# Attention rounds of a fused attention and mixture-of-experts kernel: another order of rows, transposes, evictions and sums, and an earlier start of the first expert slot's gathers

## The chip, the cores and the metric

The kernel runs on one core of one Trainium2 chip. The metric is the time of one execution on the device, in microseconds (us). Besides the timed runs there is one profiled execution, whose instructions, waits and transfers can be looked at one by one.

## What is computed

The reference has two parts. The first is attention in chunks: 8 batches, 8 heads and 576 positions of 64 numbers; each chunk of 64 positions sees only itself. The second is a layer of 8 experts: each of the 4608 rows (8 heads of 64 numbers side by side, 512 in all) goes to the one expert with the largest logit.

```python
scores = scale * np.matmul(q_c, k_c.transpose(0, 1, 2, 4, 3))
scores = scores - np.max(scores, axis=-1, keepdims=True)
attn = np.exp(scores)
attn = attn / (np.sum(attn, axis=-1, keepdims=True) + 1e-09)
out = np.matmul(attn, v_c)
...
logits = x @ w_gate + modality_bias[modality_id]
e_idx = np.argmax(logits, axis=1)
gate_w = probs[np.arange(N), e_idx]
for e in range(E):
    mask = e_idx == e
    h = np.maximum(x[mask] @ w1[e], 0.0)
    out[mask] = gate_w[mask, None] * (h @ w2[e])
```

## The kernel before, in words

The 4608 rows are 36 tiles of 128. The program order of every engine is written out by hand, so each engine runs its own queue in just the order in which the code emits instructions; waits between engines are semaphores.

**A tile of attention** passes through these helpers. `scores` multiplies q and k on TensorE (PE) into `sp` in PSUM, takes the maximum on VectorE (DVE, line 249) and subtracts it (line 251). `exps` takes the exponential `ex` on ScalarE (ACT, line 256), and GpSimd (POOL) adds its two halves into `sr` (line 257). `sums` adds these up on DVE (lines 261, 262) to the reciprocal `ris`. `transposes` turns `ex` on PE (line 268) and ACT evicts it as `at` (line 270). `values` multiplies with v on PE (line 282) and ACT evicts `xt` (line 285). `rows` turns the product back on PE (line 294, which also gives the gate's logits) and DVE scales it into `xr` (line 296). `put` copies the logits `lp` on ACT (line 306) and stores `xr` to the array `xd` in DRAM, by a DMA that ACT issues (line 307).

**A round** handles two tiles, a and a+1, from a = 2 to 34. In before it is, on PE: transposes of a, rows of a-2 and of a-1, transposes of a+1, scores of a+2 and a+3, values of a and a+1. PSUM has eight banks: four for the pair `yb`, two under the tag "s" (for `sp`) and two under "t" (for `ap`, `xp`). The exponential of a+2 is emitted straight behind the scores, the one of a+3 behind both values. Loads of v are held until a transpose of the round is done.

**Routing.** The first 14 tiles are group 0. In the rounds behind them `route` works out each row's place (DVE, POOL, and two matmuls into `rp`, line 364), and `scatter` writes 14 times 128 rows into the table `tab` (POOL indirect DMAs, line 385), one per call of `advance`. `early_table` picks the first three expert slots. `locate` then reads a slot's list from the table into `tl` (SP DMA, line 523); it waits until all 14 scatters have landed. `gather` copies the row numbers to `tk` (POOL, line 540) and fetches the rows from `xd` into `xg` (POOL indirect DMAs, line 544, one for each 128 rows). `split` transposes `xg` on PE (line 584), and ACT and DVE split it into a high and a low part (lines 585, 586).

**The table PLAN** says what of the first slot's preparation follows the values of which tile: the key k stands for tile 36 + k. "locate" and "gather" are as above, "fetch" loads weights, "hi" and "lo" split them (ACT line 612, DVE line 616).

**The expert slots** follow: 13 sure ones and a few that depend on the input. In each, eight steps of `first` (line 641) and `second` (line 654) keep PE at work. The last tile's rows are taken inside slot 0 by `last`.

Of the kernel before, what the change touches and what calls it, by code (L numbers as in the profile page):

```python
# [8 lines left out]
F32 = mybir.dt.float32  # L9
# [13 lines left out]
E = 8  # L23
# [11 lines left out]
BUSY = 4  # L35
PLAN = {
    -9: {"fetch": [(0, 1), (1, 1)]},
    -7: {"locate": [(0,), (1,), (2,)]},
# [51 lines left out]
def attention_moe(ctx: ExitStack, tc: tile.TileContext, qkv, mod, cst, bias, wcat, wfst, out):  # L90
# [23 lines left out]
    def load_v(t, hold=None):  # L114
        if t < NT:
            b = wk.tile([P, DM], F32, name="v", bufs=NV)
            d = SP.dma_start(b, qkv[t][:, 2])
            if hold is not None:
                after(d, [hold.ins.name], "loads of v while the whole array works")
            st[t]["v"] = b  # L120
# [60 lines left out]
    def clear_part():  # L181

        i = len(clears)
        if i < 2 * E:
            a, n = (0, low_rows) if i < E else (low_rows, CAP - low_rows)
            m = ROW * n // P
            w = SP.dma_start(tabe[i % E:i % E + 1, ROW * a:ROW * (a + n)].rearrange("e (p m) -> p (e m)", p=P),
                            oob[:, 0:m])
            apart(w, "tab")
            clears.append(w)  # L190
# [63 lines left out]
    def exps(t):  # L254
        ex = st[t]["ex"]
        A.activation(ex, ex, AF.Exp, scale=0.125)  # L256
        G.tensor_tensor(sring[t % 4][:, :, 0:32], ex[:, :, 0:32], ex[:, :, 32:64], ALU.add)  # L257

    def sums(t):
        sm = wk.tile([P, H], F32, name="sm")  # L260
        V.reduce_sum(sm, sring[t % 4], axis=AX.X)  # L261
        V.reciprocal(ris[:, t], sm)

    def transposes(t):
        ex = st[t]["ex"].rearrange("p h k -> p (h k)")
        ap = ps.tile([P, NP, P], F32, tag="t", name="ap")
        for p in range(NP):
            hold = PE.transpose(ap[:, p, :], ex[:, p * P:p * P + P], ident)  # L268
        at = mp.tile([P, DM], F32, tag="yo", name="at", bufs=4).rearrange("p (a c) -> p a c", a=NP)
        A.copy(at, ap)  # L270
        st[t]["at"] = at
        return hold
# [15 lines left out]
    def rows(t):  # L288
        xt, ri = st[t]["xt"], ris[:, t]

        xr = wk.tile([P, NJB, NK, 32], F32, name="xr", bufs=4)
        fp = yb[t % 2].rearrange("p b (a c) -> p (b a) c", a=2)
        for p in range(NP):
            PE.matmul(fp[:, p, 0:GWC], xt[:, p, :], gw[:, p, :], start=True, stop=True)  # L294
        rb = ri.rearrange("p (a b) -> p a b", a=NP).unsqueeze(3)
        V.tensor_tensor(  # L296
            xr.rearrange("p (b j) a d -> p a b j d", b=2),
            fp[:, :, 0:P].rearrange("p a (b j d) -> p a b j d", b=2, j=2),
            rb.unsqueeze(4).to_broadcast([P, NP, 2, 2, 32]), ALU.mult)
        st[t] = fp, xr  # L300

    def put(t):
        fp, xr = st.pop(t)
        g = next(i for i, (a, n) in enumerate(GROUPS) if a <= t < a + n)
        lp = lps[g % 2][:, t - GROUPS[g][0]]
        A.copy(lp.rearrange("p (a b) d -> p a (b d)", a=NP), fp[:, :, P:GWC])
        A.dma_start(xd[t * P:(t + 1) * P, :], xr.rearrange("p j c d -> p (j c d)"))
# [4 lines left out]
    def route(g):  # L312
        t0, n = GROUPS[g]
        ts = slice(t0, t0 + n)

        def tl(name, dt=F32, bufs=1):
            return wk.tile([P, n, E], dt, name=name, bufs=bufs)


        l0 = lps[g % 2][:, 0:n]  # L320
        (G if g < NEG else V).tensor_tensor(
            l0, l0, ris[:, ts].unsqueeze(3).to_broadcast([P, n, H, E]), ALU.mult)
        yield
        lh = wk.tile([P, n, H // 2, E], F32, name="lh", bufs=1)
        lg = tl("lg")
        G.tensor_tensor(lh, l0[:, :, 0:4], l0[:, :, 4:8], ALU.add)
        G.tensor_tensor(lh[:, :, 0:2], lh[:, :, 0:2], lh[:, :, 2:4], ALU.add)
        G.tensor_tensor(lg, lh[:, :, 0], lh[:, :, 1], ALU.add)
        G.tensor_tensor(lg, lg, mb[:, ts], ALU.add)
        for _ in range(1 if g < NEG else 5):  # L330
            yield
        mx = wk.tile([P, n], F32, name="gmx")
        V.reduce_max(mx, lg, axis=AX.X)
        V.tensor_tensor(lg, lg, bc(mx, n), ALU.subtract)
        ge = tl("ge")
        A.activation(ge, lg, AF.Exp)
        va = tl("va")
        V.scalar_tensor_tensor(va, lg, 0.0, rev.unsqueeze(1).to_broadcast([P, n, E]), ALU.is_equal, ALU.mult)
        fm = wk.tile([P, n], F32, name="fm")
        V.reduce_max(fm, va, axis=AX.X)  # L340
        yield

        off = OFF
        oh = tl("oh", BF16)
        V.tensor_tensor(oh, va, bc(fm, n), ALU.is_equal)
        V.tensor_copy(scan[0][:, off + 1:off + 1 + n], oh)
        d = 1
        i = 0
        while d < n:
            if d == 4:  # L350
                yield
            a, b = scan[i], scan[1 - i]
            V.tensor_tensor(b[:, off + 1:off + 1 + n], a[:, off + 1:off + 1 + n],
                            a[:, off + 1 - d:off + 1 - d + n], ALU.add)
            d, i = 2 * d, 1 - i
        gs = wk.tile([P, n], F32, name="gs")
        V.reduce_sum(gs, ge, axis=AX.X)
        V.tensor_scalar_add(gs, gs, 1e-9)
        tg = tgs[g]
        V.reciprocal(tg.bitcast(F32)[:, :, 1], gs)  # L360
        for _ in range(2 if g < NEG else 5):
            yield
        rp = ps.tile([P, 2, 32, E], F32, tag="t", name="rp")
        PE.matmul(rp[:, 0, 0:n], ub, oh, start=True, stop=True)
        PE.matmul(rp[:, 1, 0:n + 1], ones, scan[i][:, off:off + n + 1], start=True, stop=True)
        V.tensor_tensor(base[g + 1], base[g], rp[:, 1, n], ALU.add)
        ra = tl("ra")
        V.tensor_tensor(ra, rp[:, 0, 0:n], base[g].unsqueeze(1).to_broadcast([P, n, E]), ALU.add)
        V.tensor_tensor(ra, ra, rp[:, 1, 0:n], ALU.add)
        V.tensor_tensor(ra, ra, oh, ALU.mult)  # L370
        pf = wk.tile([P, n], F32, name="pf")
        V.reduce_sum(pf, ra, axis=AX.X)
        pi = cp.tile([P, n], I32, name=f"pi{g}")
        V.tensor_copy(pi, pf)
        if g == NEG - 1:
            jobs.append(early_table())
        elif g == len(GROUPS) - 1:
            jobs.append(slot_table())
        pooljobs.append(scatter(g, pi, tg))
# [198 lines left out]
    def split(k, tag="t"):  # L578

        hi, lo = xring[0]  # L580
        tp = ps.tile([P, 512], F32, tag=tag, name="tp")[:, 0:SLOT]
        for t in range(NTT):
            assert ("rows", 0, t) in ready
            PE.transpose(tp[:, t * P:(t + 1) * P], xg[:, t, k * P:(k + 1) * P], ident)
        A.copy(hi[:, k], tp)
        V.tensor_tensor(lo[:, k], tp, hi.bitcast(F32)[:, k], ALU.subtract)  # L586
# [153 lines left out]
    busy(BUSY)  # L740

    for a, n in [(0, 1), (1, 1)] + [(t, 2) for t in range(2, NT, 2)]:
        hold = transposes(a)
        if a > 1:
            for t in (a - 2, a - 1):
                rows(t)
                sums(t + 2)
                put(t)
            load_v(a + 2, hold)
            if 8 <= a < 24:  # L750
                clear_part()
            load_v(a + 3, transposes(a + 1))
            if 8 <= a < 24:
                clear_part()
            for g, (t0, m) in enumerate(GROUPS):
                if t0 + m == a:
                    jobs.append(route(g))
        else:
            if not a:
                exps(1)  # L760
            sums(a)
        advance([pooljobs])
        small = [t for t in (range(a + 2, a + 4) if a > 1 else (a + 2,)) if t < NT]
        for t in small:
            scores(t)
            load_qk(t + NB)
        if n == 2 and small:
            exps(a + 2)
        advance([pooljobs])
        for t in range(a, a + n):  # L770
            values(t)
            if small and (n == 1 or t > a):
                exps(small[-1])
            advance()
            plan(t - NT)
        if a == 2:
            prepare()
    split(0, "s")
    rows(NT - 2)
    split(1, "s")  # L780
    put(NT - 2)
    split(2)
    split(3)
# [81 lines left out]
```

## Time and profile before

| what | value |
|---|---|
| timed runs | 563.55, 566.1 and 566.12 us, median 566.1 |
| the profiled execution | 564.9 us, of it 563.1 us span |
| PE busy | 548.5 us, 97% |
| DVE busy | 360.9 us, 64% |
| ACT busy | 244.7 us, 43% |
| POOL busy | 173.7 us, 31% |
| granted clock of PE | 0.996 |

The span reaches from the first to the last instruction of the program. In a timeline a row is: start in us, duration in us, engine, line, operation, tiles (written<-read), shapes, count, and in brackets the idle time of the engine before it with what ended it. In the chain of waits a row is start, duration, and what the end of the program waited for at that time. An engine name with q is its sequencer, which issues DMAs. Ends of matmuls are modelled, so rounds are best measured from start to start.

### The profile page before, as it was taken

What the parts mean: (1) busy time and instruction counts of PE and PEld (TensorE: products, weight loads), DVE (VectorE), ACT (ScalarE), POOL (GpSimd) and SP (SyncE); (2) the same over time, 40 slices, a digit from 0 to 9 for tenths busy, and PEclk for the clock granted to TensorE, in tenths of its full rate; (3) what the DMA queues carried; (4) which work ended last, traced back from release to release, by engine and by line L of the source; (5) the groups of instructions that cost most, each with busy time, mean ns of one, the idle gap of its engine ahead of it and who ended that gap; (6) DMA issues with size and microseconds to landing.
All of it is one profiled execution on the core that took longest, in us unless ns stands there. A gap on an engine that the chain in (4) does not pass through costs nothing.

```text
span 563.1 us, 12401 instructions
## 1 busy us (share of the span) xinstructions
PE 548.5 (97%) x4900; PEld 497.6 (88%) x4900; DVE 360.9 (64%) x633; ACT 244.7 (43%) x422; POOL 173.7 (31%) x182
## 2 busy tenths in 40 slices
PE   8999999999999999999999999999999999999994
PEld 5999999988889899899898998998898998998993
DVE  4767798967899665655656565565655646556751
ACT  3455555556534433433434434343434434445531
POOL 3322526733558753031220402213032210402001
PEclk9999999999999999999999999999999999999998
DMA  8889999989788649787683876758486673757400
GB/s 329 317 299 320 357 343 324 303 295 366 224 267 264 211 141 312 260 242 219 166 306 125 265 248 195 252 138 286 175 262 230 177 259 113 233 186 234 161 37 26
DMA packets 61410, 133.22 MB, mean 237 GB/s; under 512 B 11231, under 2 KB 31391, under 8 KB 54945
## 3 DMA queue, kind: packets, MB, share of 16 engines
q1 hardware_dynamic: 48368, 103.08, 56.3%
q0 software_dynamic: 7072, 19.18, 10.3%
q10 hardware_dynamic: 5904, 10.11, 4.9%
q8 instruction: 40, 0.66, 0.5%
q14 instruction: 26, 0.20, 0.1%
HBM read 102.16 MB, written 30.70 MB: 236 GB/s over the span
## 4 chain that ended last, share of the span: by engine, by line
PE 73%; issue 13%; DVE 5%; POOL 3%; ACT 2%; DMA 2%; ACTq 0%; POOLq 0%; DVEq 0%
PE yb L654 29%; PE hp L641 28%; PE yb L294 5%; PE xp L282 5%; PE sp L247 4%; PE ap L268 2%; DVE xr L296 1%; POOL out L666 1%; DMA out<-yo,tk 1%; DVE ex L251 1%; DMA qk<-in_qkv 1%; DVE mx L249 1%; ACT ex L256 1%; DVE sm L261 1%; POOL xg L544 0%
## 5 line engine op out<-in xcount | busy, mean ns | idle before, releaser
L616 DVE TENSOR_TENSOR wl<-raw,wh 128x1024 fp32r<-128x1024 f32 (+1 forms) x106 | 129.6, 1224 | 37.2 <-ACT wh L612 37.1
L644 ACT ACTIVATE hh<-hp 128x384 fp32r<-128x384 f32 (+1 forms) x104 | 49.3, 474 | 217.8 <-PE hp L641 215.0
L641 PE MATMUL hp<-xl,wh 128*128 128x384 f32 (+1 forms) x416 | 136.5, 328 | 0.0
L641 PE MATMUL hp<-xh,wh 128*128 128x384 f32 (+1 forms) x416 | 136.2, 327 | 0.0
L641 PE MATMUL hp<-xh,wl 128*128 128x384 f32 (+1 forms) x416 | 136.2, 327 | 0.0
L645 DVE SCALAR_TENSOR_TENSOR hl<-hp,hh 128x384 fp32r<-128x384 f32 (+1 forms) x104 | 55.7, 536 | 111.1 <-ACT hh L644 111.0
L654 PE MATMUL yb<-wh,hl 128*128 128x512 f32 x296 | 117.3, 396 | 0.5 <-DVE hl L645 0.5
L654 PE MATMUL yb<-wh,hh 128*128 128x512 f32 x296 | 117.4, 397 | 0.0
L654 PE MATMUL yb<-wl,hh 128*128 128x512 f32 x296 | 116.7, 394 | 0.0
L666 POOL DMA_INDIRECT out<-yo,tk x37 | 46.9, 1266 | 223.5 <-DVE yo L665 215.9
L612 ACT CAST wh<-raw 128x1024 fp32r<-128x1024 f32 (+1 forms) x106 | 108.5, 1025 | 0.2 <-issue 0.2
L641 PEld LDWEIGHTS hp<-xl,wh 128*128 128x128 f32 x416 | 78.2, 188 | 4.2 <-DVE xl L586 0.3
L641 PEld LDWEIGHTS hp<-xh,wh 128*128 128x128 f32 x416 | 78.3, 188 | 3.9
L641 PEld LDWEIGHTS hp<-xh,wl 128*128 128x128 f32 x416 | 78.4, 188 | 0.0
L654 PEld LDWEIGHTS yb<-wh,hl 128*128 128x128 f32 x296 | 55.9, 189 | 14.9 <-DVE hl L645 1.4
L654 PEld LDWEIGHTS yb<-wl,hh 128*128 128x128 f32 x296 | 55.7, 188 | 9.6
L654 PEld LDWEIGHTS yb<-wh,hh 128*128 128x128 f32 x296 | 55.6, 188 | 9.0
L544 POOL DMA_INDIRECT xg<-xd,tk x37 | 41.1, 1111 | 23.5 <-issue 13.5
L257 POOL TENSOR_TENSOR sr<-ex 128x256 f32<-128x256 f32 x36 | 26.1, 726 | 71.6 <-ACT ex L256 71.5
L385 POOL DMA_INDIRECT tab<-tg,pi x36 | 39.6, 1100 | 15.0 <-issue 9.1
L282 PE MATMUL xp<-at,v 64*64 64x64 f32 x1152 | 38.1, 219 | 3.2 <-issue 2.0
L282 PEld LDWEIGHTS xp<-at,v 64*64 64x64 f32 x1152 | 35.8, 135 | 4.2 <-issue 2.4
(126 smaller groups left out, 523.1 us busy)
## 6 DMA issues: line engine op xcount, KB each, us to landing
raw<-in_wcat SPq DMA_DIRECT2D x48, 1024.0 KB, 6.2
qk<-in_qkv SPq DMA_DIRECT2D x36, 512.0 KB, 6.4
v<-in_qkv SPq DMA_DIRECT2D x36, 256.0 KB, 4.2
xd<-xr ACTq DMA_DIRECT2D x36, 256.0 KB, 4.6
xs<-xg SPq DMA_DIRECT2D x10, 768.0 KB, 6.3
xq<-xs SPq DMA_DIRECT2D x40, 192.0 KB, 4.3
raw<-in_wfst SPq DMA_DIRECT2D x4, 512.0 KB, 4.4
raw<-in_wfst SPq DMA_DIRECT2D x2, 1024.0 KB, 5.0
```

Source lines behind the costliest of these rows:

```text
L257: G.tensor_tensor(sring[t % 4][:, :, 0:32], ex[:, :, 0:32], ex[:, :, 32:64], ALU.add)
L282: PE.matmul(xp[hs, p, c * 64:c * 64 + 64], v[hs, vs], at[hs, p, c * 64:c * 64 + 64], start=True, stop=True)
L294: PE.matmul(fp[:, p, 0:GWC], xt[:, p, :], gw[:, p, :], start=True, stop=True)
L385: w = G.indirect_dma_start(tab, bass.IndirectOffsetOnAxis(ap=pi[:, j:j + 1], axis=0), tg[:, j, :], None, bounds_check=E * CAP - 1, oob_is_ ...
L544: G.indirect_dma_start(xg[:, t, :], None, xd[0:n, :], bass.IndirectOffsetOnAxis(ap=tk[:, t:t + 1], axis=0), bounds_check=n - 1, oob_is_err ...
L612: A.copy(hi, raw)
L616: (G if pool else V).tensor_tensor(lo, raw, hi.bitcast(F32), ALU.subtract)
L641: PE.matmul(hp, a[:, ks], b[:, k, 0:n], start=(m == 0), stop=(m == 3 * NK - 1))
L644: A.activation(hh[:, 0:n], hp, AF.Relu)
L645: V.scalar_tensor_tensor(hl[:, 0:n], hp, 0.0, hh.bitcast(F32)[:, 0:n], ALU.max, ALU.subtract)
L654: PE.matmul(y, a[:, tsl], b[:, DM:2 * DM], start=(f == 0 and i == 0), stop=(f == NF - 1 and i == 2))
L666: w = G.indirect_dma_start(out, bass.IndirectOffsetOnAxis(ap=tk[:, t:t + 1], axis=0), yo, None, bounds_check=N - 1, oob_is_err=False)
```

## The change

In the program of a round, PE now does rows of a-2, transposes of a, rows of a-1, transposes of a+1, and then scores and values as before. The sums of a+1 are emitted behind the scores. The exponential of a+2 is emitted behind the values of a, so ACT evicts `xt` of a ahead of it. The two matmuls `rp` of group 0 take a bank of tag "s" in place of "t". In the last round the first two of the four turns (`split`) of slot 0 stand ahead of the values of tiles 34 and 35, not behind them. In PLAN, only the first slot's list is located behind tile 29, and its first two gathers follow at once; the other two lists and the third gather come behind tile 30.

```diff
-    -7: {"locate": [(0,), (1,), (2,)]},
-    -6: {"gather": [(0, (0, 1))], "hi": [(0, 0)]},
-    -5: {"gather": [(0, (2,))], "lo": [(0, 0)], "hi": [(0, 1)]},
+    -7: {"locate": [(0,)], "gather": [(0, (0, 1))]},
+    -6: {"gather": [(0, (2,))], "locate": [(1,), (2,)], "hi": [(0, 0)]},
+    -5: {"lo": [(0, 0)], "hi": [(0, 1)]},
...
-        rp = ps.tile([P, 2, 32, E], F32, tag="t", name="rp")
+        rp = ps.tile([P, 2, 32, E], F32, tag="s" if g < NEG else "t", name="rp")
...
-        hold = transposes(a)
         if a > 1:
-            for t in (a - 2, a - 1):
-                rows(t)
-                sums(t + 2)
-                put(t)
-            load_v(a + 2, hold)
-            if 8 <= a < 24:
-                clear_part()
-            load_v(a + 3, transposes(a + 1))
-            if 8 <= a < 24:
-                clear_part()
+            for t in (a, a + 1):
+                rows(t - 2)
+                load_v(t + 2, transposes(t))
+                if t == a:
+                    sums(t)
+                put(t - 2)
+                if 8 <= a < 24:
+                    clear_part()
...
-        if n == 2 and small:
-            exps(a + 2)
+        if n == 2:
+            sums(a + 1)
+        if not small:
+            split(0, "s")
+            split(1, "s")
         advance([pooljobs])
         for t in range(a, a + n):
             values(t)
-            if small and (n == 1 or t > a):
-                exps(small[-1])
+            if small:
+                exps(small[t - a])
             advance()
             plan(t - NT)
...
-    split(0, "s")
     rows(NT - 2)
-    split(1, "s")
     put(NT - 2)
     split(2)
     split(3)
```

Three places of the order are used below. The first is ACT in a round in the middle of attention; `yb_96` is the bank of the odd tile.

```order
 L307 DMA xd<-xr 128x512
+L270 COPY at<-ap 128x512
 L306 COPY lp_131<-yb_96 128x64
 L307 DMA xd<-xr 128x512
-L270 COPY at<-ap 128x512
-L256 ACTIVATE ex<-ex 128x512
-L285 COPY xt<-xp 128x512 x2
+L285 COPY xt<-xp 128x512
+L256 ACTIVATE ex<-ex 128x512
+L285 COPY xt<-xp 128x512
 L256 ACTIVATE ex<-ex 128x512
```

The second `at` has moved ahead of the second `lp`, and the first exponential of the round has moved from ahead of both `xt` to between them.

The second place is POOL behind the last scatter, where `sr_136`, `sr_137`, `sr_134` and `sr_135` belong to tiles 30, 31, 32 and 33, and `tk_160` holds the row numbers of slot 0.

```order
 L385 DMA tab<-tg_125,pi_1653 36864x16
 L257 TENSOR_TENSOR sr_136<-ex 128x8x32
 L257 TENSOR_TENSOR sr_137<-ex 128x8x32
-L257 TENSOR_TENSOR sr_134<-ex 128x8x32
 L540 COPY tk_160<-tl_159 128x3
 L544 DMA xg<-xd,tk_160 128x512 x2
+L257 TENSOR_TENSOR sr_134<-ex 128x8x32
+L544 DMA xg<-xd,tk_160 128x512
 L257 TENSOR_TENSOR sr_135<-ex 128x8x32
-L544 DMA xg<-xd,tk_160 128x512
```

The copy of the list and the first two gathers have moved ahead of the add of tile 32, and the third gather ahead of the add of tile 33.

The third place is PE in the last round, from the transposes of tile 35 to the end of the turns.

```order
 L268 MATMUL ap<-cs,ex 128x128 x4
+L584 MATMUL tp<-cs,xg 128x128 x6
 L282 MATMUL xp<-at,v 64x64 x32
-L584 MATMUL tp<-cs,xg 128x128 x3
 L294 MATMUL yb_95<-cs,xt 128x144 x4
-L584 MATMUL tp<-cs,xg 128x128 x9
+L584 MATMUL tp<-cs,xg 128x128 x6
```

Six of the twelve turns, which need all three gathers, now stand ahead of the values of tiles 34 and 35.

More of the change, by code (lines that the diff above doesn't have):

```diff
@@ L758, in attention_moe @@
         else:
+            transposes(a)
             if not a:
```

## The prediction

> **What bounds the kernel now.** I read the busy times by stretch first, to see which engine leaves no room and where.
>
> ```profile
> 90.00:110.00 20.00, 20.00 (x452) 19.46 (x449) 18.22 (x53) 11.10 (x24) 15.01 (x17) 1.00 0.95 322
> 200.00:260.00 60.00, 60.00 (x301) 54.06 (x300) 33.93 (x45) 25.15 (x39) 19.17 (x18) 1.00 0.77 248
> ```
>
> The columns are the stretch, its length, then PE, weight loads, DVE, ACT and POOL busy, PE's granted clock, the share of the DMA engines and GB/s. PE is busy without a gap in a quiet stretch of attention and in the expert slots. The change touches attention and the start of slot 0 alone, so the expert slots keep their length, and the end of the program moves by as much as the start of slot 0 moves. What can be won is the time by which rounds of attention are longer than a quiet round. So next comes the chain of waits over attention, with the starts of rows (`yb`, line 294) as marks of a round. The first fence is its answer up to 90 us, the second the answer for the whole span.
>
> ```profile
> 14.95 1.98 PE yb L294 x16
> ...
> 20.77 0.75 issue
> ...
> 71.85 2.00 PE yb L294 x16
> ...
> 87.40 1.96 PE yb L294 x16
> ```
>
> ```profile
> 101.13 1.96 PE yb L294 x16
> ...
> 108.00 1.96 PE yb L294 x16
> ...
> 131.03 1.00 PE yb L294 x8
> ```
>
> From 101.13 to 108.00 is one quiet round, 6.87 us. The marks 14.95, 71.85, 87.40, 108.00 and 131.03 are those of a = 2, 18, 22, 28 and 34. So eight rounds up to 71.85 took 56.90 for 54.96 (1.94 over), two rounds to 87.40 took 15.55 for 13.74 (1.81 over), and three from 108.00 took 23.03 for 20.61 (2.42 over). These 6.2 us, and the passage into slot 0, are all that the change can reach.
>
> **The change, part by part.** *The order of rows and transposes in a quiet round.* The timeline of one such round:
>
> ```profile
> 100.47 0.66 PE L268 MATMUL ap<-cs,ex 128*128 128x128 f32 x4
> ...
> 100.97 2.13 PE L294 MATMUL yb<-cs,xt 128*128 128x144 f32 x16
> ...
> 102.93 0.60 PE L268 MATMUL ap<-cs,ex 128*128 128x128 f32 x4
> ...
> 103.46 2.08 PE L247 MATMUL sp<-qk 64*64 64x64 f32 x64
> ```
>
> From start to start four transposes take 0.50 us ahead of rows and 0.53 ahead of scores, and the rows of two tiles 1.96. The count stays, only the neighbours change. I take 0; if each of 17 rounds gained or lost the difference of 0.03, it would be 0.5 either way. Rows of a-2 now come first, so `xt` has no transposes to hide behind. Scores and values fill the time from 103.46 to the next round at 100.47 + 6.87 = 107.34, so the values of one tile take about 0.97, and while PE does the second tile's, ACT has 0.97 for the first one's eviction of 0.57 (row 129.75 below). That fits, with some 0.25 to spare.
>
> *Eviction ahead of the exponential, `rp` in the other tag, second sums behind the scores.* These aim at the two long rounds from 71.85. Their timeline:
>
> ```profile
> 77.66 0.63 ACT L256 ACTIVATE ex<-ex 128x512 f32<-128x512 f32 x1 [0.90 <-DVE ex L251]
> ...
> 78.19 1.05 ACT L285 COPY xt<-xp 128x512 f32<-128x512 f32 x2
> ...
> 78.81 0.66 PE L268 MATMUL ap<-cs,ex 128*128 128x128 f32 x4 [0.66 <-ACT xt L285]
> ...
> 85.04 0.57 ACT L285 COPY xt<-xp 128x512 f32<-128x512 f32 x1
> ...
> 85.66 1.15 PE L282 MATMUL xp<-at,v 64*64 64x64 f32 x32 [0.64 <-ACT xt L285]
> ```
>
> In the first, PE waited 0.66 for a bank that `xt` had not left, since `xt` stood behind an exponential which itself waited for DVE, late by the work of `route`. In the changed order `xt` waits for the values alone, so this wait goes. In the second, PE waited 0.64 for the bank that `rp` had taken out of the turn of "t"; with `rp` under "s" this goes too. The sum is 1.30 of the 1.81. What is late next is the copy `lp`, which follows DVE's `xr` on ACT; it stands a whole scores and values ahead of the next `xt`, and this cover is some 2.9 us. Bounds: 0 if DVE's lateness reaches PE through `lp`, 1.81 if both rounds become quiet. I take 1.3. Moving the second sums off the path from `xr` to the exponential gives DVE 0.6 us of air a round (0.43 and 0.20, rows 127.17 and 127.63 below); in a quiet round nobody waits for it. Of the 1.94 of the first eight rounds the largest gap shown, 0.75, is "issue": PE waited for nothing that this change touches. Bounds 0 and 1.94, I take 0.2, near the lower end.
>
> *The list alone and the gathers earlier.* The timeline of the last rounds:
>
> ```profile
> 110.98 0.99 POOL L385 DMA_INDIRECT tab<-tg,pi  x1 [0.17 <-issue]
> ...
> 116.74 3.05 SPq L523 DMA_DIRECT2D tl<-tab  x3
> ...
> 120.61 0.72 POOL L257 TENSOR_TENSOR sr<-ex 128x256 f32<-128x256 f32 x1 [4.37 <-ACT ex L256]
> ...
> 122.68 0.19 POOL L540 COPY tk<-tl 128x3 int32<-128x3 int32 x1 [1.35 <-DMA tl<-tab]
> ...
> 124.00 1.07 POOL L544 DMA_INDIRECT xg<-xd,tk  x1 [1.13 <-DMA v<-in_qkv]
> ...
> 125.37 1.01 POOL L544 DMA_INDIRECT xg<-xd,tk  x1 [0.30 <-issue]
> ...
> 126.40 0.74 POOL L257 TENSOR_TENSOR sr<-ex 128x256 f32<-128x256 f32 x1
> ...
> 127.17 0.43 DVE L261 TENSOR_REDUCE sm<-sr 128x8 f32<-128x264 f32 x1 [1.14 <-POOL sr L257]
> 127.30 1.00 POOL L544 DMA_INDIRECT xg<-xd,tk  x1 [0.16 <-issue]
> ...
> 127.63 0.20 DVE L262 RECIPROCAL ris<-sm 128x8 f32<-128x8 f32 x1
> 127.75 0.64 DVE L249 TENSOR_REDUCE mx<-sp 128x8 f32<-128x512 f32 x1
> 128.43 0.69 DVE L251 TENSOR_TENSOR ex<-sp,mx 128x512 f32<-128x512 f32 x1
> ...
> 129.21 0.63 ACT L256 ACTIVATE ex<-ex 128x512 f32<-128x512 f32 x1 [1.98 <-DVE ex L251]
> 129.75 0.57 ACT L285 COPY xt<-xp 128x512 f32<-128x512 f32 x1
> ...
> 130.22 0.62 ACT L612 CAST wh<-raw 128x512 fp32r<-128x512 f32 x1
> ...
> 132.83 0.60 PE L268 MATMUL ap<-cs,ex 128*128 128x128 f32 x4
> ...
> 136.06 0.55 PE L584 MATMUL tp<-cs,xg 128*128 128x128 f32 x3
> ...
> 137.95 0.48 ACT L585 CAST xh<-tp 128x384 fp32r<-128x384 f32 x1 [0.81 <-PE tp L584]
> ...
> 140.84 1.14 PE L294 MATMUL yb<-cs,xt 128*128 128x144 f32 x8
> ```
>
> The reader should see the path of the 2.42 us: the last scatter leaves at 110.98, the lists are asked for when it has landed, at 116.74, and POOL stands until 122.66 for the first of them. The view of tile `tl` says how long it took:
>
> ```profile
> DMA to landing us min/median/max: 5.9/5.9/5.9
> ```
>
> By the Trainium skill ("DMA: Bandwidth & Descriptors", section "Anatomy of one DMA — SWDGE (gpsimd) path") a DMA takes about 2.0 us plus its bytes at 436 GB/s, so these 3 KB would land in 2.0 us; the trace's 5.9 disagrees, and the sum goes by the 5.9.
>
> In before the copy and two gathers (122.68 to 126.38) delayed the add of tile 33 until 126.40, DVE's sums until 127.17, and then maximum, exponential and `xt`. The list was already the first of the three that SP asked for, so asking for it alone does not bring it sooner; the scatter ahead of it stands behind the same add as before. So POOL's copy and gathers run at the same time, but now they stand ahead of the add of tile 32, which had run at 120.61. That add ends at 127.14. Queued behind it: sums of tile 32 to 127.8 (0.43 and 0.20), then `xr` of tile 31, which in before was done earlier (some 0.69, as a subtraction in row 128.43), maximum and subtraction to 129.85, exponential to 130.5 on ACT, the cast 0.62, `xt` of tile 33 to 131.75, its rows 0.98, and the transposes of tile 35, 0.53, which end at 133.3. In before they end at 132.83 + 0.53 = 133.36. So this wait is moved, not removed: I take 0. The moved sums pay for the worse place. Bounds: -2.42 if the list comes sooner, +0.7 if the `xr` that waits now also holds back `xt` through `lp`.
>
> *Two turns ahead of the last values.* They need all three gathers. The third left at 127.30, just behind the delayed add, and it leaves just behind the delayed add again. The view of tile `xg` from 80 to 160 us gives the landing of its transfers:
>
> ```profile
> DMA to landing us min/median/max: 4.3/6.9/9.5
> ```
>
> So it lands at 131.6 to 136.1 (in before the turns at 136.06 did not wait for it, which is a bound), by the median at 134.2. PE reaches the turns at 133.3 and waits 0.9 (0 to 2.8). Then PE has twelve turns of about 0.13, two values of 1.07, rows 0.98 and the first twelve matmuls of the slot, 2.1: 6.8 us, so 141.0. The low part of the last turns hangs on ACT, where `xh` (0.48) of turns 2 and 3 stands behind the `lp` of tile 34; some 0.2 more, 141.2. Before was at the same place at 140.84. I take +0.35, bounds -0.7 and +2.2.
>
> *The rest.* Locating the other two lists later, the loads of v held by the same transposes, and the new order of the stores of `xd` cost nothing: slot 1's gather waits for the turns (`xg` is still in use), and a quiet round has a whole round between a load and its use. If that cover went, a late v would hold the values by what its load is late.
>
> **The sum.** -1.3 - 0.2 + 0 + 0.35 = -1.15 us against the profiled execution's 564.9, that is 563.75. The three timed runs have a median of 566.1 and go from 563.55 to 566.12; the middle of all four executions is 565.5, and 1.2 less is 564.3, which I give.
>
> **The rivals.** *The list comes soon enough.* If the lists land faster with less asked for at a time, the gathers fit into the 4.37 us in which POOL stood idle ahead of 120.61. The shortest landing that the page shows is this one:
>
> ```profile
> xq<-xs SPq DMA_DIRECT2D x8, 128.0 KB, 2.6
> ```
>
> With 2.6 the copy starts at 119.4, the gathers end at 123.1 and the add of tile 32 at 123.85. In an unhindered sequence the round a = 32 starts at 121.74, and with rows 0.98 and `xr` 0.69 its sums are wanted at about 123.5, so almost nothing is left of the wait: -2.4, the turns find their rows (-0.7), and in all -4.6, or 560.9. The fit of the Trainium skill (the page "DMA: Bandwidth & Descriptors" and its section named above) would have the list here sooner still. For it: three lists of 8-byte pieces are asked for at once. Against: the one we need was first in the queue. Chance 0.20.
>
> *The turns hold up the last values.* PE works in order, so a late third gather now stops values, rows and slot 0, where in before it could come as late as 136.06. At a landing of 9.5 (the longest in the row) it arrives at 136.8; PE waits 3.5, slot 0 is late by 3.2, and after the gain of 1.5 the kernel is 1.7 slower, 567.2. It decides from a landing of 135.4 on, where the gain is used up. For it: weight loads leave on SP in the same time, right behind the last v. Against: in before it had landed by 136.06 in the same crowd. Chance 0.10.
>
> *Nothing changes.* DVE late by `route` finds another way to PE, and the gaps come back one engine further: 565.5. Chance 0.12; the forecast has 0.58.
>
> **How the numbers follow.** About 0.5%, 2.8 us, is what a measurement of this kernel can tell from no change. The forecast and "nothing changes" lie within it, the first rival outside. With a tenth of the forecast's own width beyond 2.8 us: faster 0.26, slower 0.07 (half of the second rival and a little of the forecast), same 0.67. The range is 561.0 to 567.1: from the first rival's time to the second's.
>
> **What would show it.** Right, if in the new profile the rounds a = 18 and 20 have no wait of PE for `xt` over 0.2 us, quiet rounds stay at 6.87, POOL's copy of the list waits for `tl` with the add of tile 32 behind it, DVE waits for that `sr` by some 3 us, and PE waits at the first turn for `xg`. Wrong, if the copy finds its list at once, if quiet rounds change their length, or if PE waits for `xt` at the start of every round, which would mean that the 0.25 us of air are not there.

## The result, and the profile after

The changed kernel takes 571.5 us (median of 12 runs, 568.25 to 574.62) where the kernel before takes 565.7 (12 runs, 563.55 to 568.19): 1.0109 times as long, interval 1.0091 to 1.0128. The forecast was 564.3, and the range ended at 567.1. The profiled execution has a span of 568.0 us, 4.9 more than before. All ratios here and below are of fast runs alone; of e6 below, half of the ten runs, the profiled one among them, were slow and are not in its ratio.

These are rows of the chain of waits of the changed kernel (start, duration, what).

```profile
98.83 1.18 PE yb L294 x8
...
105.74 1.18 PE yb L294 x8
...
118.52 6.07 DMA tl<-tab
...
127.93 8.72 DMA xg<-xd,tk
...
137.63 3.26 PE xp L282 x64
```

A quiet round is 6.91 us, from 98.83 to 105.74; before it was 6.87. Two transfers now stand in the chain, a list and the third gather, where before it ran over DVE, ACT and POOL. The same place in the timeline of the changed kernel:

```profile
114.64 0.40 SPq L523 DMA_DIRECT2D tl<-tab  x1
...
123.33 0.18 POOL L540 COPY tk<-tl 128x3 int32<-128x3 int32 x1 [8.63 <-DMA tl<-tab]
...
124.32 2.08 PE L247 MATMUL sp<-qk 64*64 64x64 f32 x64
...
124.97 1.41 SPq L601 DMA_DIRECT2D raw<-in_wfst  x3
...
127.04 0.73 POOL L257 TENSOR_TENSOR sr<-ex 128x256 f32<-128x256 f32 x1
127.81 0.43 DVE L261 TENSOR_REDUCE sm<-sr 128x8 f32<-128x264 f32 x1 [4.54 <-POOL sr L257]
127.93 1.02 POOL L544 DMA_INDIRECT xg<-xd,tk  x1 [0.16 <-issue]
...
129.07 0.21 ACT L306 COPY lp<-yb 128x64 f32<-128x64 f32 x1 [4.01 <-DVE xr L296]
...
130.09 1.25 PE L294 MATMUL yb<-cs,xt 128*128 128x144 f32 x8 [1.82 <-ACT xt L285]
...
132.13 1.25 PE L294 MATMUL yb<-cs,xt 128*128 128x144 f32 x8 [0.33 <-ACT xt L285]
...
135.00 0.33 PE L584 MATMUL tp<-cs,xg 128*128 128x128 f32 x1 [1.07 <-DMA xg<-xd,tk]
...
136.70 0.93 PE L584 MATMUL tp<-cs,xg 128*128 128x128 f32 x4 [1.38 <-DMA xg<-xd,tk]
...
137.56 3.33 PE L282 MATMUL xp<-at,v 64*64 64x64 f32 x64
...
142.49 0.42 PE L641 MATMUL hp<-xh,wh 128*128 128x384 f32 x1
```

Read it from the top. SP asks for the list 2.1 us sooner than before (114.64, not 116.74), but the copy starts at 123.33, later than the 122.68 of before. POOL stands for it, the add of tile 32 behind it runs at 127.04, DVE waits 4.54, and PE gets `xt` 1.82 late. The third gather leaves at 127.93, lands 8.72 us later, and PE goes on at 136.70. At the turns it waits 1.07 and 1.38. Then the 64 matmuls of the last values take 3.33 us; in a quiet round they take 2.03. The view by stretches tells why:

```profile
133.53:136.94 3.41, 0.96 (x7) 0.53 (x6) 2.68 (x7) 1.01 (x3) 0.48 (x1) 1.00 0.94 377
136.94:140.35 3.41, 3.41 (x56) 3.08 (x56) 1.12 (x2) 1.73 (x4) 0.00 (x0) 0.50 0.15 55
```

The column behind POOL's is the granted clock. In 3.41 us PE was busy for 0.96, and in the next 3.41 us it got half its clock.

I use one measure below, the **passage**: from the start of the last scores (tiles 34 and 35) to slot 0's first matmul. Here it is 142.49 - 124.32 = 18.17 us. In the kernel before the same two rows start at 125.52 and 138.32: 12.80. So the sum of the profile is: 1.2 gained up to the last scores, 5.4 lost in the passage, 0.7 lost behind it (of it 0.5 after the last matmul), 4.9 in all.

### The profile page after: what moved, and what is told of

Read it like the earlier page. It is cut to its first block, busy times and chain, and to the rows that moved or that the text cites. A ratio compares the mean times of both kernels' runs of the same rounds, so it can differ in the third digit from the quotient of the medians.

```text
span 568.0 us, 12434 instructions
## 1 busy us (share of the span) xinstructions
PE 551.6 (97%) x4900; PEld 500.3 (88%) x4900; DVE 364.0 (64%) x633; ACT 244.0 (43%) x422; POOL 174.0 (31%) x182
## 4 chain that ended last, share of the span: by engine, by line
PE 78%; issue 12%; DMA 3%; DVE 2%; POOL 2%; ACT 1%; ACTq 0%; SPq 0%; POOLq 0%; DVEq 0%
PE yb L654 29%; PE hp L641 29%; PE yb L294 6%; PE sp L247 6%; PE xp L282 5%; PE ap L268 2%; DMA xg<-xd,tk 2%; DVE wl L616 1%; DMA tl<-tab 1%; POOL out L666 1%; DMA raw<-in_wcat 1%; PE yb L166 1%; POOL xg L544 0%; DVE ex L251 0%; DVE mx L249 0%
## 5 line engine op out<-in xcount | busy, mean ns | idle before, releaser
L294 PE MATMUL yb<-cs,xt 128*128 128x144 f32 x288 | 43.3, 293 | 2.6 <-ACT xt L285 2.6
L294 PEld LDWEIGHTS yb<-cs,xt 128*128 128x128 f32 x288 | 37.3, 190 | 4.3 <-ACT xt L285 3.2
```

## The experiments

The runs e1 to e4, e5 to e8, e9 to e12, e13 to e15, and e16 with e17 shared a chip each, with runs of the kernel before beside them. The table has their times, and of the traces the passage, the third gather from leaving to landing (the last step of its semaphore), PE's waits at the turns for gathers (all in us), and the windows at half clock ahead of slot 0.

| run | time to before (interval) | passage | third gather | PE waits | half clock |
|---|---|---|---|---|---|
| before, first profile | 1 | 12.80 | 7.8 | 0 | 0 |
| changed, first profile | 1.0109 (1.0091 to 1.0128) | 18.17 | 8.7 | 2.4 | 1 |
| e1 turns back | 1.0101 (1.007 to 1.0131) | 14.88 | 9.4 | 0.2 | 1 |
| e2 table back | 1.0176 (1.0113 to 1.0238) | 19.00 | 9.2 | 3.3 | 2 |
| e3 round only | 1.0100 (1.007 to 1.013) | 11.56 | 7.2 | 0 | 3 |
| e4 before, turns ahead | 1.0031 (1.0009 to 1.0052) | 13.00 | 7.9 | 0.6 | 0 |
| e5 changed again | 1.0058 (1.0012 to 1.0103) | 18.62 | 8.8 | 2.5 | 2 |
| e6 changed, scatters spaced | 0.9976 (0.9924 to 1.0028) | 19.30 | 9.5 | 3.2 | 1 |
| e7 round, scatters spaced | 1.0006 (0.9961 to 1.0052) | 11.96 | 7.7 | 0 | 0 |
| e8 before, scatters bunched | 0.9939 (0.9901 to 0.9978) | 12.85 | 7.1 | 0 | 0 |
| e9 changed, PE kept busy | 1.0092 (1.0069 to 1.0115) | 17.88 | 9.2 | 0.9 | 0 |
| e10 changed, four blocks not loaded | one run, 564.4 | 14.68 | 8.7 | 2.6 | 0 |
| e11 transposes first | 1.0046 (1.0029 to 1.0064) | 14.23 | 8.6 | 1.9 | 0 |
| e12 before again | one run, 564.2 | 12.69 | 8.1 | 0 | 0 |
| e13 changed, loads held | 1.0020 (1.0002 to 1.0037) | 14.57 | 4.0 | 0 | 0 |
| e14 as e7 | 1.0005 (0.9984 to 1.0026) | 15.88 | 8.8 | 2.0 | 1 |
| e15 as e3 | 1.0025 (1.0002 to 1.0047) | 16.78 | 8.8 | 2.6 | 1 |
| e16 as e7, loads held | 0.9973 (0.9951 to 0.9995) | 11.50 | 4.5 | 0 | 0 |
| e17 before, loads held | 1.0002 (0.9978 to 1.0025) | 12.38 | 5.4 | 0 | 0 |

**Each part undone (e1 to e4).** e1 and e2 undo one part of the changed kernel, e3 both, e4 is the kernel before with one part done:

```diff
# e1 (and e3): turns behind the values again
-        if not small:
-            split(0, "s")
-            split(1, "s")
...
+    split(0, "s")
     rows(NT - 2)
+    split(1, "s")
# e2 (and e3): PLAN of before
-    -7: {"locate": [(0,)], "gather": [(0, (0, 1))]},
...
+    -7: {"locate": [(0,), (1,), (2,)]},
...
```

> The changed kernel with only the two turns put back behind the last values. Theory A (turns): PE, which works in order, stands 1.07 and 1.38 us at the turns for the second and third gather, and its values then take 3.33 us for 64 matmuls at half the granted clock where 2.03 is usual; with the values ahead of the turns both go, so slot 0's first matmul comes near 139 instead of 142.49 and the time falls by 3 to 4 us, to about 568 beside 571.5. Theory B (lists): the loss is made by POOL's copy, which waits 8.6 us for the list ahead of the add of tile 32; the values then only find the same lateness and the time falls by at most 1.5 us, to 570.

> The changed kernel with only the table of due times put back (three lists located together, copy and two gathers a round later, third gather behind the next add). Theory A (turns): PE gets to the turns sooner, but the third gather still leaves behind an add near 127 and lands near 135, so the wait at the turns stays or grows (2.4 to 3.5 us) and the time falls by at most 1.5 us, to 570 or more. Theory B (lists): the wait of PE for xt in the round a = 32 falls from 2.15 us to 0.9 or less and the delay behind it goes too; the time falls by 3 us or more, to 568 or less.

> The changed kernel with both the turns and the table put back, so that only the new order inside a round is left (rows ahead of each turn of transposes, eviction ahead of the exponential, second sums behind the scores, the other tag for rp). Theories A and B together: all of the loss lies in the passage into slot 0, and the round itself gained 1.6 us up to a = 30, so the time is 1 to 2 us below the kernel before, 564 to 565 beside 565.7. Rival: the round's order itself makes later rounds worse (each round is 0.04 longer and the last rounds are late): then the time is not below that of before.

> The kernel before with only the two turns moved ahead of the last values. Theory A (turns): PE reaches the turns at 133.4 and the third gather lands at 135.05, so it waits about 1.7 us, and whatever the granted clock loses behind that comes on top (up to 1.3); less 0.47 of a wait that goes, 1 to 2.5 us slower, 566.7 to 568.2 beside 565.7. Theory B (lists): the turns cost nothing of their own, within 0.5 us of the kernel before.

By the times neither theory holds: e1, e2 and e3 were all 1% or more slower than before, even with the round alone, and the kernel before itself took 569.6 us beside them. The traces show something that the first profiles had not. These are e1's rows of PE, and of POOL's scatters:

```profile
92.89 0.98 POOL L385 DMA_INDIRECT tab<-tg,pi  x1 [0.30 <-issue]
...
93.62 0.35 PE L282 MATMUL xp<-at,v 64*64 64x64 f32 x5 [0.39 <-issue]
...
94.17 0.98 POOL L385 DMA_INDIRECT tab<-tg,pi  x1 [0.30 <-issue]
94.35 0.36 PE L282 MATMUL xp<-at,v 64*64 64x64 f32 x5 [0.38 <-issue]
95.08 0.36 PE L282 MATMUL xp<-at,v 64*64 64x64 f32 x4 [0.36 <-issue]
```

Behind POOL's scatters, PE gets some five matmuls per 0.73 us; these gaps are the pauses spoken of below. From the scores of tile 24 to those of tile 34 e3 took 46.4 us, where the kernel before took 35.8 in its first profile. So these total times say little on the passage, but the passage itself can be read from each trace. With the new round and the turns ahead it is 18 to 19 us (e2, and the changed kernel), with the turns back 14.9 (e1), with both back 11.6 (e3). In the old round the turns ahead cost 0.2 (e4, 13.00). So theory A holds for the changed kernel, and the lists cost some 2 to 3 us beside it; but the turns are harmful only where the gathers land late for PE.

**Scatters in a row (e5 to e8).** In the new round the exponential of a+2 stands behind the values of a, so POOL's add of that tile does too, and the scatters fall three and one between the adds instead of two and two. That is POOL's order in a piece of the kernel before and of the changed one, as adds (a) and scatters (S): `SSaSSaSSa` and `SSSaSaSSSaSa`. e6 and e7 space them again; e8 bunches them in the kernel before:

```diff
# e6, e7
-        advance([pooljobs])
         small = ...
...
             advance()
+            if t == a:
+                advance([pooljobs])
# e8 (kernel before)
             values(t)
+            if t == a + 1:
+                advance([pooljobs])
             if small and (n == 1 or t > a):
                 exps(small[-1])
-            advance()
+            advance([jobs] if t == a + 1 else None)
```

> The changed kernel as it is, beside the next three. All theories: 5 to 6 us slower than the kernel before. Theory C (scatters in a row): the move of the exponentials lets three of POOL's scatters of the token table follow each other where there were two (order of adds and scatters 3, 1, 3, 1 instead of 2, 2, 2, 2); behind the second scatter in a row PE gets only about 5 matmuls per 0.73 us, and where that fills enough of one 3.41 us window, the next window runs at half the granted clock, which costs 1.7 us. So here a window at half clock or pauses of PE called issue between 90 and 115 us, or both; without such pauses in this run, only the passage into slot 0 is late, as in the first profile.

> The changed kernel with the scatters two and two again (one call that lets POOL's jobs advance is moved from ahead of the scores to behind the first values). Theory C (scatters in a row): no window at half clock between 90 and 120 us and at most three groups of pauses in a row; 2 to 5 us faster than the changed kernel of this call where that one shows pauses, equal where it shows none. Theory D (the round's order itself, rows in two groups of eight): no difference to the changed kernel over 1 us.

> Only the new order inside a round (turns and table as in the kernel before), and the scatters two and two. Theory C (scatters in a row): the 5.6 us that the round's order alone cost go, since neither three scatters in a row nor the passage into slot 0 is left, and the gain up to a = 30 is seen: 0.5 to 2 us faster than the kernel before. Theory D (the round's order itself): still 3 us or more slower than the kernel before.

> The kernel before with only its scatters bunched three and one (one call that lets POOL's jobs advance is moved from behind the second values' exponential to ahead of it); nothing else is moved on PE, ACT or DVE. Theory C (scatters in a row): longer pauses of PE between 90 and 115 us, one or more windows at half clock there, 3 to 5 us slower than the kernel before. Theory D (the round's order itself): within 0.5 us of the kernel before.

The kernel before took 576.3 us beside these, from 568.9 to 578.4, with PE's pauses in all four traces. In the new round, spacing left two or three pauses in a row where there had been up to four, and no window at half clock ahead of the last scores (e6 and e7; e1, e2, e3 and e5 had one to three). But e8, bunched, had no such window either and was not slower (its 0.9939 stands beside a kernel before that spread over 10 us, and its passage shows no gain). So theory C holds in part at most: bunching makes the pauses denser in the new round, and the rest of it fell with e8.

**The clock, the crowd, the round (e9 to e12).**

```diff
# e9: ten matmuls that nobody reads, ahead of the turns
+            air = ps.tile([P, 512], F32, tag="s", name="air")
+            for _ in range(10):
+                PE.matmul(air, warm[:, 0:P], warm, start=True, stop=True)
             split(0, "s")
# e10: the buffer as it is in place of a load, at -9, -4 and -3
-    -9: {"fetch": [(0, 1), (1, 1)]},
+    -9: {"keep": [(0,), (1,)]},
...
# e11 (on e7): the transposes of a ahead of rows again, as on PE before
+                if t == a:
+                    hold = transposes(t)
                 rows(t - 2)
...
```

> The changed kernel with ten more matmuls of 512 columns, on a bank that nobody reads, ahead of the first turn; they do no part of the computation. The passage is counted from the start of tile 34's scores to slot 0's first matmul: 18.2 to 19.3 us in three runs of the changed order, 12.8 in the kernel before. Theory A with the clock (the wait for the gathers leaves PE so idle that the next 3.41 us run at half the granted clock): the ten matmuls take about 2.2 us out of a wait of 2.4 to 3.2, no window at half clock follows, and the passage is 1.0 to 1.7 us shorter, 16.5 to 17.8. Rival (the clock falls for another reason, or the values were slow for want of data): still half clock for 3.41 us, and the passage stays at 18.2 or gets longer by the part of the ten matmuls that the wait doesn't cover.

> The changed kernel without the loads of the first four blocks of weights (2 MB, due at -9, -4 and -3; the buffers are set to zero at the start, so slot 0 computes with zeros there). Theory E (crowd): the list took 8.2 to 9.0 us and the third gather 8.7 to 9.5 us to land since they stand in the same DMA engines behind these loads and those of qk; without the weights the list lands in 6.5 us or less, the third gather in 6 us or less, PE waits under 0.5 us at the turns, there is no window at half clock, and the passage falls from 18.2 to 15 us or less. Rival (the gathers are slow by themselves or leave too late): landing times over 8 us and a wait of 2 us or more stay.

> The kernel before with what proved harmless: turns and table as before, the matmuls of PE in the very order of before, but eviction ahead of the exponential, second sums behind the scores, rp in the other tag, and the scatters two and two. All theories: quiet rounds of 6.87 us, the two long rounds from a = 18 shorter by 1.3, the passage 12.0 to 12.8. On a chip without pauses 1 to 2 us faster than the kernel before; with pauses (as in the last two calls) the gain can be lost in their spread, but not turn into a loss over 1 us.

> The kernel before as it is, for a profile on the chip of this call. If pauses of PE behind two of POOL's scatters in a row belong to the chip, they are here as in the other runs of this call (on a chip like that of the first profiles: none), two or three at a time, and no window at half clock falls between 10 and 550 us.

None of these four traces has the pauses, and the kernel before took 564.5. e9's timeline:

```profile
135.18 2.32 PE L770 MATMUL air<-warm 128*128 128x512 bf16 x9
...
138.67 0.66 PE L584 MATMUL tp<-cs,xg 128*128 128x128 f32 x4 [0.95 <-DMA xg<-xd,tk]
139.25 2.08 PE L282 MATMUL xp<-at,v 64*64 64x64 f32 x64
...
142.92 0.42 PE L641 MATMUL hp<-xh,wh 128*128 128x384 f32 x1
```

The values take 2.08 again, and no window at half clock follows. From the third gather (138.67) to slot 0 are 4.25 us; in the changed kernel 142.49 - 136.70 = 5.79. So the half clock costs 1.5 us, as expected. The passage fell by 0.3 alone, since this time the gather landed 1.2 us later after the start of the scores (138.62 - 125.04 = 13.58; in the changed kernel 136.65 - 124.32 = 12.33), and the time shows no gain.

In e10, which leaves out the loads of four blocks, the first half came as expected and the second did not:

```profile
113.94 0.42 SPq L525 DMA_DIRECT2D tl<-tab  x1
...
119.15 0.18 POOL L542 COPY tk<-tl 128x3 int32<-128x3 int32 x1 [4.50 <-DMA tl<-tab]
...
124.18 1.02 POOL L546 DMA_INDIRECT xg<-xd,tk  x1 [0.16 <-issue]
124.33 12.56 SPq L603 DMA_DIRECT2D raw<-in_wfst  x2
...
132.91 0.66 PE L586 MATMUL tp<-cs,xg 128*128 128x128 f32 x4 [2.63 <-DMA xg<-xd,tk]
```

Without 1 MB of weights ahead of it the list is there in 5.2 us, not 8.7. But the third gather still took 8.7: a load of 1 MB that was left, asked for at 124.33, left right beside it (the second load of that row was asked for at 136.5). So 1 MB beside the gather held it up as long as the 2 MB of the changed kernel. e11 was expected to be faster and was 0.46% slower. The view of waits names the reason: with the exponential behind `xt`, transposes that stand first wait for it in 14 rounds. So the change's order of rows ahead of transposes is needed by its order on ACT.

```profile
PE ap L268 <- ACT ex L256: 3.9, 14, 0.3
```

**The loads held back (e13 to e17).**

```diff
# e13 (on the changed kernel), e16 (on e7), e17 (on the kernel before); w is the load
...
+        if 2 <= g <= 4:
+            after(w, gathers[2:3])
```

> The changed kernel with one wait more: the loads of the weight blocks 2 to 5 (2 MB, due at -4, -3 and -1) are asked for when the third gather of the first slot has landed, instead of beside it. Theory E' (the third gather shares the DMA engines with these loads; without the first four blocks it still took 8.7 us beside the 1 MB of blocks 4 and 5): it lands within 6 us of leaving instead of 8.7, PE waits 1 us or less at the turns, no window at half clock follows, the passage from the start of tile 34's scores to slot 0's first matmul falls from 18.2 to 15 us or less, and the time by 3 us or more. Rival (a third gather in a row is slow by itself): still over 8 us, a wait of 2 us and more, no gain; the weights then come later still and slot 0 waits for them.

> Only the new order inside a round, scatters two and two, turns and table as before (as in the seventh run, beside other kernels). If the round's order is a gain of its own: the passage takes 11.5 to 12.0 us, tile 34's scores start at the same time as in the kernel before or up to 1.6 us sooner, and the kernel is 0.5 to 2 us faster than the one before on a chip without pauses. If the round's order costs by itself what the turns and the table cost in this document's account: 1 us or more slower.

> The same with the scatters three and one, as the change has them, on the chip of the run above. Theory C (scatters in a row): on a chip with pauses four of them in a row, a window at half clock behind them and 2 to 4 us slower than with two and two; on a chip without pauses no difference. Rival (the bunching doesn't matter, the spread between runs made it look so): no difference on either.

The timeline of e13, whose line numbers are one or two higher:

```profile
127.66 1.02 POOL L545 DMA_INDIRECT xg<-xd,tk  x1 [0.16 <-issue]
...
129.81 1.25 PE L294 MATMUL yb<-cs,xt 128*128 128x144 f32 x8 [1.53 <-ACT xt L285]
...
131.72 1.42 SPq L603 DMA_DIRECT2D raw<-in_wfst  x3
...
131.85 1.25 PE L294 MATMUL yb<-cs,xt 128*128 128x144 f32 x8 [0.34 <-ACT xt L285]
...
133.38 0.82 PE L586 MATMUL tp<-cs,xg 128*128 128x128 f32 x6
...
137.24 1.25 PE L294 MATMUL yb<-cs,xt 128*128 128x144 f32 x8 [0.70 <-ACT xt L285]
```

The held loads leave when the third gather has landed, at 131.72: 4.06 us after it left, instead of 8.7. PE does the six turns in one piece. The passage is 14.57, 3.6 less than in the changed kernel, and the time is 1.0020 of before instead of 1.0109. So theory E' holds: it was the loads beside the gather. e14 and e15, with turns and table of before, were a surprise: their rounds brought PE to the turns sooner (134.42 in e14, 136.06 before), the gather landed later (137.0, before 135.05), and there PE waited for it, as e14 shows.

```profile
128.19 1.01 POOL L544 DMA_INDIRECT xg<-xd,tk  x1 [0.16 <-issue]
...
137.06 0.33 PE L584 MATMUL tp<-cs,xg 128*128 128x128 f32 x1 [2.04 <-DMA xg<-xd,tk]
```

The round's gain was eaten there, wherever the turns stood. e14 and e15 don't differ beyond their intervals, so without pauses the bunching costs nothing that can be told.

> The new order inside a round, scatters two and two, turns and table as before, and the loads of the weight blocks 2 to 5 held until the third gather has landed. Theory E' (the gather shares the DMA engines with these loads): the third gather lands in 4 to 6 us, ahead of the turns, PE waits for it under 0.3 us, no window at half clock follows, and the passage takes 11.5 to 12.2 us; with the start of tile 34's scores 0.4 to 1.4 us sooner than before, 1 to 2.5 us faster than the kernel before. Rival (the weights now come too late): slot 0's first matmul as early as that, but then waits of PE for wl or wh, and no gain.

> The kernel before with the same loads held, nothing else. In it the gathers land 1 us ahead of the turns already, so the held loads have nothing to win: within 1 us of the kernel before, and if slower, by the weights that come late. If it is faster by as much as the run beside it, the gain there belongs to the held loads and not to the round.

e16 is the version that the experiments point to: 562.7 us beside 564.7 for the kernel before, ratio 0.9973 with an interval that ends at 0.9995. It is the only version with the new round that is clear of the kernel before on the fast side, and only just. Its timeline:

```profile
127.55 1.01 POOL L545 DMA_INDIRECT xg<-xd,tk  x1 [0.16 <-issue]
...
132.09 2.73 SPq L603 DMA_DIRECT2D raw<-in_wfst  x4
...
133.26 0.55 PE L586 MATMUL tp<-cs,xg 128*128 128x128 f32 x3
...
135.52 0.42 PE L645 MATMUL hp<-xh,wh 128*128 128x384 f32 x1
```

The gather has landed by 132.09, ahead of the turns, and the passage is 11.50. The held loads by themselves win nothing (e17, 1.0002). So by this one set of runs the round's order is worth about 0.3% once the gather no longer takes it back.

## Why the prediction was wrong

*Quiet round, 0.* It is 0.04 longer, 0.7 over 17 rounds; slightly over the bound of 0.5. `xt` has the 0.25 of air that was counted on: no round waits for it but those below.

*Rounds 18 and 20, -1.3.* PE still waits 0.41 for `xt` once, behind the `ge` of `route` on ACT, at 72.18, so of the two waits of 1.30 a net 0.9 goes. From the scores of tile 18 to those of tile 24 the changed kernel takes 21.8 us, where before it was 22.4, so about 0.65 arrived, half of what was forecast.

```profile
71.36 0.30 ACT L336 ACTIVATE ge<-lg 128x112 f32<-128x112 f32 x1 [0.97 <-DVE lg L334]
...
72.18 1.25 PE L294 MATMUL yb<-cs,xt 128*128 128x144 f32 x8 [0.41 <-ACT xt L285]
```

In part "nothing changes" was right here: DVE's lateness by `route` found another way.

*First eight rounds, -0.2.* In the first pair of profiles this was -1.4. But the gaps are waits of PE named issue, and they differ from run to run of one kernel: the seven rounds from the scores of tile 4 to those of tile 18 took 50.0 us in the first profile of the kernel before and 48.8 in e12. In profiles without pauses the last scores start at 124.45 on average with the new round (the changed kernel, e9, e13 to e16; 124.02 to 125.04), and at 125.43 with the old (before, e12, e17; 124.55 to 126.23). So the rounds gain about 1.0 (the two groups overlap by a little), and the forecast's -1.5 was near.

*The list, 0.* This failed in size. That the copy and the gathers would hold up the add of tile 32 was right; that the list would be there at 122.68 was not (123.33), and the wait for `xt` that follows is 2.15 in two pieces where before it was 0.91. The list was asked for 2.1 us sooner, but the weights ahead of it had left at the same time as before (109.74, before 109.75); e10, which leaves these out, has only the second piece, 0.33. e13, which has neither wait at the turns nor half clock, still has a passage of 14.57. That is 1.8 more than before, and 3.1 more than e16, whose loads are held too but whose turns and table are those of before (and whose scatters are spaced). Of the 3.1, 2.6 are waits of PE for `xt`, and e16 has none of them: 1.53 and 0.34 ahead of the turns, which belong to this step, and 0.70 behind them. So this step cost about 1.9, where 0 was put. (The 2.0 us that the prediction sets beside the list is, by the name of the section that it cites, for the gpsimd path; SP asks for this list, and in the runs it took 5 to 9 us.)

*Two turns ahead of the last values, +0.35.* This is the step that failed most. It took the median landing of 6.9, so 134.2, a wait of 0.9. The gather took 8.7, and PE waited 2.45. That by itself is the second rival, "the turns hold up the last values", which was to decide from a landing of 135.4 on; it landed at 136.7. What no step had is the second price: the idle PE then ran at half clock, 1.5 us more. e13 takes both away, 3.6 us in the passage and about 0.9% in time (1.0020 against 1.0109, in different sets of runs).

Two causes lie under this step. The first is the row of landings, 4.3/6.9/9.5, which was read as a spread to take the middle of. It holds only two landings, both of gathers of later slots. The same view, narrowed to the gather that left at 139.10, has the smaller one:

```profile
L544 POOL DMA_INDIRECT xg<-xd,tk x1: 1030/1030/1030, 139.1 to 139.1; - x1
...
DMA to landing us min/median/max: 4.3/4.3/4.3
```

The other left at 156.28 and took 9.5. For slot 0's own gathers the view prints no landing, so 6.9 is the middle of two transfers that the step isn't about. The third gather's semaphore shows 7.8 in the kernel before (the table). Put into the same sum, that is a wait of 1.75 and a gain of 0.3 in place of 1.15. And what crowded the gather could be seen: SP's loads of weights, which now leave at 124.97, ahead of the second gather (126.00), where in the kernel before they left behind it:

```profile
125.37 1.01 POOL L544 DMA_INDIRECT xg<-xd,tk  x1 [0.30 <-issue]
...
126.15 1.59 SPq L601 DMA_DIRECT2D raw<-in_wfst  x3
```

The second cause: the gather of before was said to have landed in the same crowd by 136.06. That is true, with 1 us to spare, which the faster rounds needed themselves.

The second rival's sum has a slip: at a wait of 3.5 the step's own terms make slot 0 late by 2.95 (0.35 + 3.5 - 0.9), not 3.2, and the kernel 1.45 slower, not 1.7. The measured loss is far beyond either.

Not settled: where the last us of the measured 5.9 lies, since the profiles differ by 4.9; and what sets off the pauses of PE.

## What to carry to other kernels

Before an operation that needs a transfer is moved to the front of an in-order engine, look up what else is asked of the DMA engines in the same microseconds, and hold back what isn't needed yet; asking sooner for the small transfer does nothing while the large ones stand ahead of it. A gain upstream arrives only if the next transfer also comes sooner, so check its slack in microseconds. Price a wait of PE with the clock that follows it. And before the middle of a summary row is taken as a price, look up how many transfers the row holds and which.

## What the runs showed of the hardware

**Half clock after a thin window.** All windows at half clock ahead of slot 0 last 3.41 us or twice that. The first of e3, with the stretch ahead of it:

```profile
91.47:94.88 3.41, 2.17 (x53) 1.72 (x48) 1.42 (x3) 0.21 (x1) 2.80 (x3) 1.00 1.01 341
94.88:98.30 3.42, 3.15 (x48) 2.84 (x47) 2.45 (x6) 1.12 (x3) 0.59 (x2) 0.50 0.96 299
98.30:101.71 3.41, 3.41 (x15) 3.40 (x16) 2.22 (x10) 1.40 (x3) 2.91 (x4) 0.50 0.16 62
```

The Trainium skill ("TensorE: Matmul & The Clock Gate", section "Part 1: The HAM clock gate (the "warmup" mystery)") has a free-running window of 3413 ns, after which an idle PE gets half its clock. The trace agrees in the length, but the window need not be idle: PE was busy for 0.96 us of it in the changed kernel, and by modelled ends for 2.17 here.

**Pauses that come and go.** e3 and e15 are one kernel on one chip; from the scores of tile 24 to those of tile 34 they took 46.4 and 35.7 us. PE's pauses behind two of POOL's indirect DMAs in a row, which make the difference, belong neither to the kernel nor to the chip.

**Blocks of the program.** PE stops at one place of the program again and again: in the values of a = 30, with 27 of 64 matmuls to go, for 1.53 us in the changed kernel and 0.51 in e16.

```profile
120.33 1.03 PE L282 MATMUL xp<-at,v 64*64 64x64 f32 x27 [1.53 <-issue]
```

By the Trainium skill ("Runtime: NRT & Kernel Launch", section "Instruction fetch mechanics") an engine's program comes in blocks of 256 instructions, and the cost at a block's end is mostly hidden. Here it isn't: a stop of this kind lasts 0.2 to 2.4 us. The traces agree on the 256: the stops that end 1.2 to 1.5 us after a 16 KB packet of the instruction queue stand, counted in PE's matmuls and weight loads, at the 706th, 1218th, 1986th, 2242nd, 2754th, 5058th and a few more places, all whole multiples of 256 apart to within one.
